# Summing kv over tokens in four column tiles, and moving query, keys and additions within a chunk: a tuned attention and GELU kernel on one core

## The chip, the cores and the metric

The kernel runs on one core of a Trainium2 chip. The metric is the device time of one execution in microseconds (us), the median of several. In what follows PE is TensorE (the matrix engine), DVE is VectorE, ACT is ScalarE, POOL is GpSimd and SP is SyncE, which here issues transfers. The time before is 283.5 us, the median of 3 runs (283.37 to 283.89). A run is called slow when it is over 1.5% above the fastest of its kernel.

## The reference, cut to what matters

Attention with sketched features, and behind it a two-layer network with exact GELU. All data is float32.

```python
# q, k, v: (4 batches, 4 heads, 1088 tokens, 32);  S1, S2: (8, 32)
def phi(x):                                   # 64 features of a token
    a = np.einsum('rd,bhsd->bhsr', S1, x)
    b = np.einsum('rd,bhsd->bhsr', S2, x)
    return np.einsum('bhsi,bhsj->bhsij', a, b).reshape(*x.shape[:-1], r * r)
q_p, k_p = (phi(q), phi(k))
kv = np.einsum('bhsf,bhsd->bhfd', k_p, v)
z = np.sum(k_p, axis=2)
num = np.einsum('bhsf,bhfd->bhsd', q_p, kv)
den = np.einsum('bhsf,bhf->bhs', q_p, z)[..., None] + 1e-06
x = (num / den)                               # rearranged to (4352 tokens, 128)
# then: h = x @ w_in (128 x 2048);  g = 0.5*h*(1+erf(h/sqrt(2)));  out = g @ w_out (2048 x 128)
```

## The kernel before

The kernel works through nine chunks of tokens: eight of 512 (two to a batch) and a half-wide one made of what is left over of the four batches. A chunk has 16 steps. A step is one *hidden* product (128 columns of `w_in`), its GELU on ACT, and *output* products with `w_out`. From chunk 2 on, the output products are of a cheaper form that adds up pieces in two accumulators (3.01 us of PE in the four steps from 128.86 to 135.31, against 0.86 us a step before chunk 2); POOL makes sums of GELU results for it (`token_sums`), and at the end of a chunk the accumulators are *drained* by DVE and ACT and put together by some additions on DVE (`combine`). Between these steps the attention of the chunks to come is worked in: a query is turned, expanded to features and multiplied with kv and z (`attend`), and the keys of a batch are turned, expanded and summed to kv and z.

kv and z before came from one product: `v_aug` holds v in 32 of 64 columns and ones in the others.

```python
def kv_sum(b, ps, r):
    for i in range(J):                                    # J = 8 groups of 128 tokens
        ch, t, one = (...)                                # cut: which slice of k_p
        for c in range(NP):                               # NP = 2
            pe.matmul(ps[c * 64:(c + 1) * 64, r * F:(r + 1) * F], lhsT=v_aug[:, 2 * c + r, i, :],
                      rhs=k_p[b, r][:, t, c * 4 + ch * 2 + one].rearrange("p i j -> p (i j)"),
                      start=(r == 0 and i == 0), stop=False, skip_group_check=True)

def combine(n):                                           # chunk n is complete
    dve.tensor_copy(out=N[:, 0], in_=acc[n][0])           # the drain ...
    act.copy(out=N[:, 1], in_=acc[n][1])
    act.copy(out=C[lo, 0], in_=flat[hi, HW:3 * HW])
    dve.tensor_add(...)                                   # ... and 7 additions, cut
```

The schedule names the step at which a part is issued. On each engine the instructions run in the order of this text.

```python
for b in range(1, B):
    t = NCH * b * NF - (0 if b == 1 else 1)               # NF = 16 steps, NCH = 2
    ...
    at(t - 18, key_turn_blocks, b, r)                     # for both r
    at(t - 17, features, b, r)
    t = NCH * b * NF - (0 if b == 1 else 2)
    at(t - 14, finish_keys, b)                            # kv_sum, and the copy to kv_T by DVE
    at(t - 13, lambda b=b: turn_kv(b, held["kv"], by_dve))   # the transpose of kv on PE
for n in range(2, NCHUNK):
    t = n * NF
    early = 0 if n == 2 else -1 if n == 3 else 2
    at(t - 13 - early, query_turn, n)
    at(t - 12 - early, query_expand, n)                   # half of the expansion ...
    at(t - 11 - early, expand_finish, n, 1)               # ... and the other half
    at(t - 8, attend, n)
# cut
    hidden(n, fi, ...)
    for n in done[t]:                                     # step 5 of the next chunk
        store(n)                                          # combine, transpose, stores
    token_sums(...)
    for f in slots[t]: f()
    for f, *a in products[t]: f(*a)
```

Of the kernel before, what the change touches and what calls it, by code (L numbers as in the profile page):

```python
# [16 lines left out]
def kernel(  # L17
# [21 lines left out]
    F = R * R  # L39
# [177 lines left out]
    kz = [big.tile([128, NP, 2 * D], FP, name=f"kz{b}") for b in range(B)]  # L217

    v_aug = big.tile([128, H, J, 2 * D], FP, name="v_aug")
# [9 lines left out]
    dve.memset(v_aug, 1.0)  # L229
# [81 lines left out]
    def widen_v(b, r):  # L311
        to = v_aug.rearrange("p (c r) j (s d) -> p c r j s d", r=2, s=2)[:, :, r, :, r, :]
        pool.tensor_copy(out=to, in_=main["v", b][:, r::2])

# [58 lines left out]
    def kv_sum(b, ps, r):  # L373

        for i in range(J):

            ch, t, one = (i % 2, i // 4, i // 2 % 2) if b else (i // 4, i // 2 % 2, i % 2)
            for c in range(NP):
                pe.matmul(ps[c * 64:(c + 1) * 64, r * F:(r + 1) * F], lhsT=v_aug[:, 2 * c + r, i, :],  # L379
                          rhs=k_p[b, r][:, t, c * 4 + ch * 2 + one].rearrange("p i j -> p (i j)"),  # L380
                          start=(r == 0 and i == 0), stop=False, skip_group_check=True)

    def kv_sum_rem(b, ps):
        for r in range(2):
            for c in range(NP):
                pe.matmul(ps[c * 64:(c + 1) * 64, r * F:(r + 1) * F], lhsT=v_rem_aug[b][:, 2 * c + r, :],
                          rhs=k_p_rem[b % 2][:, 2 * c + r].rearrange("p i j -> p (i j)"),
                          start=False, stop=True, skip_group_check=True)
# [56 lines left out]
    def expand_finish(n, i):  # L445
        for g in range(2):
            expand_copy(n, 2 * i + g)
        expand_multiply(n, i)

    def query_expand(n):  # L450
        expand_products(n)
        expand_finish(n, 0)

    def attend(n):

        W = width[n]
        owners = [(0, W, n // NCH)] if n < NMAIN else [(i * REM, (i + 1) * REM, i % 2 * 2 + i // 2) for i in range(B)]
        banks = halves(work_banks())
        for (c0, c1, b) in owners:
            for c in range(NP):  # L460
                for r in range(2):
                    pe.matmul(banks[r][c * F:(c + 1) * F, c0:c1], lhsT=kz[b][r * F:(r + 1) * F, c, :],  # L462
                              rhs=qp[n][r * F:(r + 1) * F, c, c0:c1], start=True, stop=True)
        den = att.tile([128, CW], FP, name="den")
        for h in range(H):
            c, r = h // 2, h % 2
            at = c * F + (1 - r) * D
            act.activation(out=den[h * D:(h + 1) * D, :W], in_=banks[r][at:at + D, :W], func=ACT.Copy, bias=1e-6)  # L468
        dve.reciprocal(out=den[:, :W], in_=den[:, :W])  # L469
        xT[n] = att.tile([128, CW], FP, name="xT", bufs=3)  # L470
        for h in range(H):
            rows = slice(h * D, (h + 1) * D)
            dve.tensor_mul(out=xT[n][rows, :W], in0=banks[h % 2][rows, :W], in1=den[rows, :W])  # L473
# [117 lines left out]

    def combine(n):

        N = att.tile([128, 2, CW], FP, name="A_sb", bufs=2)
        C = att.tile([128, 2, CW], FP, name="A_sb", bufs=2)
        dve.tensor_copy(out=N[:, 0], in_=acc[n][0])  # L596
        act.copy(out=N[:, 1], in_=acc[n][1])
# [69 lines left out]
    widen_v(0, 0)  # L667
# [3 lines left out]
    widen_v(0, 1)  # L671
# [9 lines left out]
    kv_sum(0, kv_bank, 0)  # L681
# [4 lines left out]
    kv_sum(0, kv_bank, 1)  # L686
# [59 lines left out]
    def finish_keys(b):  # L746
        held["kv"] = work_bank()
        for r in range(2):
            kv_sum(b, held["kv"], r)
# [16 lines left out]
    for b in range(1, B):  # L766

        t = NCH * b * NF - (0 if b == 1 else 1)
        for r in range(2):
            at(t - 20, widen_v, b, r)  # L770
        at(t - 20, widen_v_rem, b)
        for r in range(2):
            at(t - 18, key_turn_blocks, b, r)
        for r in range(2):
            at(t - 17, features, b, r)
        if b == 1:
            at(t - 16, turn_keys_rem, b)
            at(t - 15, features_rem, b)
        t = NCH * b * NF - (0 if b == 1 else 2)
        at(t - 14, finish_keys, b)  # L780
        at(t - 13, lambda b=b: turn_kv(b, held["kv"], by_dve))
    for n in range(2, NCHUNK):
        t = n * NF
        early = 0 if n == 2 else -1 if n == 3 else 2
        at(t - 13 - early, query_turn, n)
        at(t - 12 - early, query_expand, n)
        at(t - 11 - early, expand_finish, n, 1)
        at(t - 8, attend, n)
# [3 lines left out]
    done = {t: [] for t in range(len(steps) + LAG + 1)}  # L792
    for t, (n, fi) in enumerate(steps):
# [9 lines left out]
        elif fi % NB == NB - 1:  # L803
# [5 lines left out]
            if b == NF // NB - 1:  # L809
                done[t + 6].append(n)  # L810

    for t in range(len(steps) + LAG):
# [4 lines left out]
        if t == 4:  # L817
            turn_x(1, work_bank())
            for f, *a in products[t]:
                f(*a)  # L820
        if t < len(steps):
            n, fi = steps[t]
            hidden(n, fi, by_halves=n >= FAST and (n < NMAIN or fi < 5))
        for n in done[t]:
            store(n)
        if t < len(steps) and FAST <= steps[t][0] < NMAIN and steps[t][1] % NB == NB - 1:
            token_sums(steps[t][0], steps[t][1] // NB)
        for f in slots[t]:
            f()
        if t != 4:  # L830
# [43 lines left out]
```

## Time and profile before

The prediction below shows the main lines of this profile. This table cuts the span at starts of hidden products on PE.

| stretch | us |
|---|---|
| start, to the first hidden product | 18.57 |
| the next 24 steps (chunks 0 and 1 in turn), with kv of batch 1 | 47.36 |
| the last 8 steps of chunks 0 and 1, and chunks 2 and 3 | 74.12 |
| chunks 4 and 5 | 62.54 |
| chunks 6 and 7 | 55.88 |
| the last, narrow chunk and the tail | 22.93 |

How to read the lines: in a view in order of time, the columns are the start and the length in us, the engine, the line of the kernel, the operation, output and inputs, the tile or shape, and how many instructions were put together; a bracket at the end tells how long the engine had stood idle and what released it. SPq is SP's queue of transfers that it issues. Lengths of products overlap: the hidden product at 128.86 before is 1.03 us long, and the next group starts 0.86 us after it. Start-to-start distances are what PE pays.

In order of time on PE before, kv of batch 1, and the one large product that keeps PE busy in the start:

```profile
52.76 2.08 PE L379 MATMUL w_ps<-k_p,v_aug 128*64 128x64 f32 x64
54.67 0.40 PE L386 MATMUL w_ps<-k_p_rem,v_rem_aug 128*64 128x64 f32 x8
55.01 1.12 PE L624 MATMUL o_ps<-g,w_out 128*128 128x512 f32 x2
...
11.67 0.70 PE L653 MATMUL h_ps<-idle 128*128 128x256 f32 x2
```

kv of batch 1 takes 2.25 us from its first product to the next group (52.76 to 55.01).

### The profile page before, as it was taken

Reading aid. Unit: us, or ns where it says so; the run is one execution under the profiler, and the core shown is the slowest. Engines: PE = TensorE matmul, PEld = TensorE weight load, DVE = VectorE, ACT = ScalarE, POOL = GpSimd, SP = SyncE. Lnnn points to the kernel's source line nnn. Section 1 sums busy time; section 2 is a strip of 40 time slices with the busy share of each in tenths; the row PEclk is TensorE's granted clock in tenths of the full one; section 3 lists DMA queues with packets and bytes.
Section 4 is the critical chain, followed back from the end, with each engine's and each line's share of the span. In section 5 each row is a group of like instructions: output and inputs, shape, how many; then the busy total and the mean of one; then the engine's idle time right before and its main releaser. Section 6 shows DMA issues by size and latency. Waiting matters only on the chain.

```text
span 281.4 us, 5436 instructions
## 1 busy us (share of the span) xinstructions
PE 273.1 (97%) x2161; PEld 138.4 (49%) x2161; DVE 169.9 (60%) x244; ACT 141.1 (50%) x270; POOL 146.5 (52%) x160
## 2 busy tenths in 40 slices
PE   8989999999999999999999979999999999999994
PEld 6744444533432447444444446444544444455893
DVE  5987788253812394369816994379717971793050
ACT  4683864266426733466346532556355634553441
POOL 3331039002005858386767786286768676867500
PEclk9999999999999999999999999999999999999998
DMA  6559343626012100000200020000100020002011
GB/s 208 183 172 309 99 116 71 171 65 160 8 25 34 19 2 2 0 2 0 41 0 0 3 37 2 0 2 7 33 0 0 2 37 3 0 0 40 1 22 37
DMA packets 37914, 13.49 MB, mean 48 GB/s; under 512 B 28288, under 2 KB 37248, under 8 KB 37888
## 3 DMA queue, kind: packets, MB, share of 16 engines
q1 hardware_dynamic: 37648, 13.05, 18.2%
q8 instruction: 17, 0.28, 0.4%
q10 hardware_dynamic: 240, 0.08, 0.1%
q14 instruction: 9, 0.07, 0.1%
HBM read 10.90 MB, written 2.23 MB: 47 GB/s over the span
## 4 chain that ended last, share of the span: by engine, by line
PE 85%; DVE 9%; ACT 3%; issue 2%; DVEq 0%
PE h_ps L518 36%; PE o_ps L589 23%; PE o_ps L624 10%; PE w_ps L419 3%; PE w_ps L621 3%; PE w_ps L379 2%; PE w_ps L462 2%; ACT A_sb L426 2%; PE w_ps L653 1%; PE w_ps L345 1%; DVE den L469 1%; DVE q_pT L440 1%; DVE xT L473 1%; PE o_ps L379 1%; DVE A_sb L596 1%
## 5 line engine op out<-in xcount | busy, mean ns | idle before, releaser
L518 PE MATMUL h_ps<-xT,w_in 128*64 128x512 f32 (+3 forms) x490 | 140.2, 576 | 1.1 <-DVE xT L501 1.0
L525 ACT ACTIVATE block<-h_ps 128x512 f32<-128x512 f32 (+1 forms) x112 | 63.4, 566 | 89.3 <-PE h_ps L518 86.9
L560 POOL TENSOR_TENSOR bits_a<-block 128x512 f32<-128x512 f32 x24 | 30.9, 1287 | 68.6 <-ACT block L525 68.6
L518 PEld LDWEIGHTS h_ps<-xT,w_in 128*64 128x64 f32 (+1 forms) x490 | 44.1, 146 | 37.1 <-issue 16.8
L589 PE MATMUL o_ps<-block,w_out 128*64 128x256 f32 x192 | 50.9, 383 | 0.0
L440 DVE TENSOR_TENSOR q_pT<-A_sb,w_ps 64x512 f32<-64x512 f32 x32 | 22.1, 691 | 32.1 <-ACT A_sb L426 31.7
L589 PEld LDWEIGHTS o_ps<-block,w_out 128*64 128x64 f32 x192 | 25.0, 137 | 31.6 <-issue 24.6
L624 PE MATMUL o_ps<-g,w_out 128*128 128x512 f32 x64 | 33.4, 603 | 0.0
L563 POOL TENSOR_TENSOR bits_m<-block,bits_e 128x512 f32<-128x512 f32 x24 | 30.9, 1286 | 1.9
L562 POOL TENSOR_TENSOR bits_e<-bits_a,block 128x512 f32<-128x512 f32 x24 | 31.5, 1314 | 0.0
L561 POOL TENSOR_TENSOR bits_low<-block 128x512 f32<-128x512 f32 x24 | 31.5, 1312 | 0.0
L525 ACT ACTIVATE g<-h_ps 128x512 f32<-128x512 f32 x32 | 19.1, 596 | 24.2 <-PE h_ps L518 24.2
L469 DVE RECIPROCAL den<-den 128x512 f32<-128x512 f32 (+1 forms) x7 | 21.7, 3094 | 8.6 <-ACT den L468 8.6
L589 PE MATMUL o_ps<-bits_low,small 128*64 128x256 f32 x96 | 26.0, 383 | 0.0
L589 PE MATMUL o_ps<-block,small 128*64 128x256 f32 x96 | 24.9, 382 | 0.3
L589 PE MATMUL o_ps<-bits_a,small 128*64 128x256 f32 x96 | 25.0, 383 | 0.0
L589 PE MATMUL o_ps<-bits_m,w_out 128*64 128x256 f32 x96 | 25.0, 383 | 0.0
L589 PEld LDWEIGHTS o_ps<-block,small 128*64 128x64 f32 x96 | 12.7, 137 | 17.2 <-issue 9.1
L426 ACT COPY A_sb<-w_ps 64x512 f32<-64x512 f32 (+1 forms) x36 | 18.3, 554 | 3.2 <-PE w_ps L419 2.9
L473 DVE TENSOR_TENSOR xT<-w_ps,den 32x512 f32<-32x512 f32 (+1 forms) x28 | 18.2, 648 | 1.0
L624 PEld LDWEIGHTS o_ps<-g,w_out 128*128 128x128 f32 x64 | 11.3, 190 | 14.2 <-issue 13.3
L468 ACT ACTIVATE den<-w_ps 32x512 f32<-32x512 f32 (+1 forms) x28 | 15.6, 558 | 2.4 <-PE w_ps L462 2.0
(151 smaller groups left out, 317.4 us busy)
## 6 DMA issues: line engine op xcount, KB each, us to landing
block<-in_moe_w_in_dram SPq DMA_DIRECT2D x3, 512.0 KB, 6.6
block<-in_moe_w_out_dram SPq DMA_DIRECT2D x3, 512.0 KB, 9.6
k<-in_k_dram SPq DMA_DIRECT2D x48, 32.0 KB, 1.8
v<-in_v_dram SPq DMA_DIRECT2D x3, 512.0 KB, 4.5
q<-in_q_dram SPq DMA_DIRECT2D x24, 64.0 KB, 3.6
out_dram<-oT SPq DMA_DIRECT2D x24, 64.0 KB, 2.2
k<-in_k_dram SPq DMA_DIRECT2D x2, 256.0 KB, 3.1
q<-in_q_dram SPq DMA_DIRECT2D x2, 256.0 KB, 4.5
```

The lines of the kernel that those rows point to most:

```text
L426: act.copy(out=A[g // 2][F:, g % 2, :width[n]], in_=B_of[n][g // 2][:F, g % 2, :width[n]])
L440: dve.tensor_mul(out=cols[r * F:(r + 1) * F], in0=a[:, :, r::2], in1=b[:, :, r::2])
L469: dve.reciprocal(out=den[:, :W], in_=den[:, :W])
L473: dve.tensor_mul(out=xT[n][rows, :W], in0=banks[h % 2][rows, :W], in1=den[rows, :W])
L518: pe.matmul(ps[rows, :W], lhsT=w[:, rows], rhs=xT[n][:, :W], start=True, stop=True)
L525: act.activation(out=g_of[n, fi][:, :W], in_=ps[:, :W], func=ACT.Gelu)
L560: pool.tensor_add(out=s[1], in0=a21, in1=a22)
L561: pool.tensor_sub(out=s[3], in0=a11, in1=a21)
L562: pool.tensor_sub(out=s[2], in0=s[1], in1=a11)
L563: pool.tensor_sub(out=s[4], in0=a12, in1=s[2])
L589: pe.matmul(acc[n][bank][half * 64:(half + 1) * 64, col:col + HW], lhsT=fixed, rhs=moving, start=b == 0 and i in (0, 2), stop=b == NF // N ...
L624: pe.matmul(o_of[n], lhsT=w_tile(w_out_sb, fi), rhs=g, start=first, stop=final)
```

## The change

The intent has four parts. (1) kv is taken from v alone, in tiles of 32 columns, four beside each other on PE. z comes from ones times the features, and for batches 1 to 3 the features are first summed over groups of tokens (`add_tokens`, on POOL for batch 1 and on DVE for batches 2 and 3), so that fewer products of ones are needed. (2) The accumulators are drained ahead of the hidden product's GELU at step 5, and the additions come at step 11, last in it. (3) The numerators (`attend`) are at step 5 of every chunk, with the keys turned between them and the reciprocal. (4) The query is turned at step 1 and expanded wholly in step 2.

```diff
-    v_aug = big.tile([128, H, J, 2 * D], FP, name="v_aug")
+    ones = big.tile([128, D], FP, name="ones")
@@
+    def add_tokens(b, r, eng):
+        ... # cut: k_s[r] is k_p summed over its halves: 128x512, then 128x256
+        eng.tensor_add(out=..., in0=kp[:, 0]..., in1=kp[:, 1]...)
+        eng.tensor_add(out=k_s[r][:, :, 0], in0=k_s[r][:, :, 0], in1=k_s[r][:, :, 1])
+
+    def kv_sum(b, ps, heads, summed=False):
+        for i in range(J):
+            for add_ones in (False,) if summed else (False, True):
+                for h in heads:
+                    kv_product(ps, ones if add_ones else main["v", b][:, h, i, :], ...)   # 32 columns
+        if summed:
+            for m in range(2):
+                for h in heads:
+                    kv_product(ps, ones, k_s[r][:, c, 0, m], h, 2 * c + 1 - r)
@@ attend
+        meanwhile()                       # the keys are turned here
         dve.reciprocal(out=den[:, :W], in_=den[:, :W])
@@ the start, batch 0
-    kv_sum(0, kv_bank, 0)
+    kv_sum(0, kv_bank, range(0, H, 2))   # not summed: 64 products where there were 32 (both halves)
@@ the schedule
+    for n in range(3, NCHUNK):
+        t = (n - 1) * NF
+        keys = n % 2 and b < B
+        at(t + 1 if n > 3 else t - 3, query_turn, n)
+        at(t + 2 if n > 3 else t - 2, query_expand, n)
+        at(t + 5, attend, n, lambda b=b, keys=keys: [key_turn_blocks(b, r) for r in range(2) if keys])
+        if keys:
+            at(t + 10, features, b, r)
+            at(t + 10, add_tokens, b, r, dve)
+            at(t + 14, finish_keys, b)
+            at(t + 15, lambda b=b: turn_kv(b, held["kv"], by_dve))
@@
-                done[t + 6].append(n)
+                drains[t + 6].append(n)
+                done[t + 12].append(n)
@@ a step
+        for n in drains[t]:
+            drain(n)
         hidden(...)
-        for n in done[t]:
-            store(n)
         token_sums(...)
         for f in slots[t]:
             f()
+        for n in done[t]:
+            store(n)
```

More of the change, by code (lines that the diff above doesn't have):

```diff
@@ L228 @@
     dve.memset(idle, 0.0)
-    dve.memset(v_aug, 1.0)
+    dve.memset(ones, 1.0)
     class Rounding:
@@ L309 @@
     kT, k_p, k_p_rem, kv_T = {}, {}, {}, {}
-    def widen_v(b, r):
-        to = v_aug.rearrange("p (c r) j (s d) -> p c r j s d", r=2, s=2)[:, :, r, :, r, :]
-        pool.tensor_copy(out=to, in_=main["v", b][:, r::2])
     def widen_v_rem(b):
@@ L371, in key_features_rem @@
         dve.tensor_mul(**spread(k_p_rem[pair], a, ab[:, :, R:2 * R]))
-    def kv_sum(b, ps, r):
+    k_s = {}
+    def add_tokens(b, r, eng):
+        words = mlp.tile([128, LC], U32, name="bits_r")
+        k_s[r] = words.bitcast(FP).rearrange("p (c two one f) -> p c two one f", c=NP, two=2, one=2)
+        kp = k_p[b, r].rearrange("p t (c two one) i j -> p t c two one (i j)", c=NP, two=2)
+        eng.tensor_add(out=k_s[r].rearrange("p c two one f -> p (c two one f)"),
+                       in0=kp[:, 0].rearrange("p c two one f -> p (c two one f)"),
+                       in1=kp[:, 1].rearrange("p c two one f -> p (c two one f)"))
+        eng.tensor_add(out=k_s[r][:, :, 0], in0=k_s[r][:, :, 0], in1=k_s[r][:, :, 1])
@@ L375, in kv_sum, with kv_product @@
+    def kv_product(ps, lhsT, rhs, h, at, start=False, stop=False):
+        r = h % 2
+        pe.matmul(ps[at * D:(at + 1) * D, r * F:(r + 1) * F], lhsT=lhsT, rhs=rhs, start=start, stop=stop,
+                  skip_group_check=True)
+    def kv_sum(b, ps, heads, summed=False):
         for i in range(J):
             ch, t, one = (i % 2, i // 4, i // 2 % 2) if b else (i // 4, i // 2 % 2, i % 2)
-            for c in range(NP):
-                pe.matmul(ps[c * 64:(c + 1) * 64, r * F:(r + 1) * F], lhsT=v_aug[:, 2 * c + r, i, :],
-                          rhs=k_p[b, r][:, t, c * 4 + ch * 2 + one].rearrange("p i j -> p (i j)"),
-                          start=(r == 0 and i == 0), stop=False, skip_group_check=True)
@@ L383, in kv_sum_rem @@
-    def kv_sum_rem(b, ps):
-        for r in range(2):
-            for c in range(NP):
-                pe.matmul(ps[c * 64:(c + 1) * 64, r * F:(r + 1) * F], lhsT=v_rem_aug[b][:, 2 * c + r, :],
-                          rhs=k_p_rem[b % 2][:, 2 * c + r].rearrange("p i j -> p (i j)"),
-                          start=False, stop=True, skip_group_check=True)
+            for add_ones in (False,) if summed else (False, True):
+                for h in heads:
+                    c, r = h // 2, h % 2
+                    kv_product(ps, ones if add_ones else main["v", b][:, h, i, :],
+                               k_p[b, r][:, t, c * 4 + ch * 2 + one].rearrange("p i j -> p (i j)"),
+                               h, 2 * c + 1 - r if add_ones else h, start=i == 0 and (summed or r == 0))
@@ new lines, in kv_sum @@
+        if summed:
+            for m in range(2):
+                for h in heads:
+                    c, r = h // 2, h % 2
+                    kv_product(ps, ones, k_s[r][:, c, 0, m], h, 2 * c + 1 - r)
+    def kv_sum_rem(b, ps):
+        for s in range(2):
+            for h in range(H):
+                c, r = h // 2, h % 2
+                side = (r + s) % 2
+                kv_product(ps, v_rem_aug[b][:, h, side * D:(side + 1) * D],
+                           k_p_rem[b % 2][:, h].rearrange("p i j -> p (i j)"), h, 2 * c + side, stop=True)
@@ L443, in expand_multiply, with attend @@
                     dve.tensor_mul(out=cols[r * F:(r + 1) * F, g], in0=a[:, g, r::2], in1=b[:, g, r::2])
-    def expand_finish(n, i):
-        for g in range(2):
-            expand_copy(n, 2 * i + g)
-        expand_multiply(n, i)
     def query_expand(n):
         expand_products(n)
-        expand_finish(n, 0)
-    def attend(n):
+        for g in range(4):
+            expand_copy(n, g)
+            if g % 2:
+                expand_multiply(n, g // 2)
+    def attend(n, meanwhile=lambda: None):
         W = width[n]
@@ L590, in two_products, with drain, combine @@
                       start=b == 0 and i in (0, 2), stop=b == NF // NB - 1, skip_group_check=True)
-    def combine(n):
-        N = att.tile([128, 2, CW], FP, name="A_sb", bufs=2)
-        C = att.tile([128, 2, CW], FP, name="A_sb", bufs=2)
+    drained = {}
+    def drain(n):
+        N, C = (att.tile([128, 2, CW], FP, name="sums") for i in range(2))
         dve.tensor_copy(out=N[:, 0], in_=acc[n][0])
         act.copy(out=N[:, 1], in_=acc[n][1])
+        drained[n] = N, C
+    def combine(n):
+        N, C = drained[n]
         flat = N.rearrange("p a b -> p (a b)")
@@ L666 @@
     query_turn(0)
-    widen_v(0, 0)
     banks = [out_bank(), out_bank()]
@@ L670 @@
     key_features(0, 1, [hidden_bank(), hidden_bank()], by_pool=(1,))
-    widen_v(0, 1)
     widen_v_rem(0)
@@ L685 @@
     expand_multiply(0, 1)
-    kv_sum(0, kv_bank, 1)
+    kv_sum(0, kv_bank, range(1, H, 2))
     keep_busy(1, hidden_bank())
@@ L747, in finish_keys @@
         held["kv"] = work_bank()
-        for r in range(2):
-            kv_sum(b, held["kv"], r)
+        kv_sum(b, held["kv"], range(H), summed=True)
         kv_sum_rem(b, held["kv"])
@@ L765 @@
         at(22 + i, channel_sums, i)
-    for b in range(1, B):
-        t = NCH * b * NF - (0 if b == 1 else 1)
-        for r in range(2):
-            at(t - 20, widen_v, b, r)
-        at(t - 20, widen_v_rem, b)
-        for r in range(2):
-            at(t - 18, key_turn_blocks, b, r)
-        for r in range(2):
-            at(t - 17, features, b, r)
-        if b == 1:
-            at(t - 16, turn_keys_rem, b)
-            at(t - 15, features_rem, b)
-        t = NCH * b * NF - (0 if b == 1 else 2)
-        at(t - 14, finish_keys, b)
-        at(t - 13, lambda b=b: turn_kv(b, held["kv"], by_dve))
-    for n in range(2, NCHUNK):
-        t = n * NF
-        early = 0 if n == 2 else -1 if n == 3 else 2
-        at(t - 13 - early, query_turn, n)
-        at(t - 12 - early, query_expand, n)
-        at(t - 11 - early, expand_finish, n, 1)
-        at(t - 8, attend, n)
+    b, t = 1, NCH * NF
+    at(t - 20, widen_v_rem, b)
+    for r in range(2):
+        at(t - 18, key_turn_blocks, b, r)
+    for r in range(2):
+        at(t - 17, features, b, r)
+        at(t - 17, add_tokens, b, r, pool)
+    at(t - 16, turn_keys_rem, b)
+    at(t - 15, features_rem, b)
+    at(t - 13, finish_keys, b)
+    at(t - 12, lambda: turn_kv(1, held["kv"], by_dve))
+    at(t - 13, query_turn, 2)
+    at(t - 11, query_expand, 2)
+    at(t - 8, attend, 2)
+    for n in range(3, NCHUNK):
+        t = (n - 1) * NF
+        b = (n + 1) // 2
+        keys = n % 2 and b < B
[3 more added lines that the diff above has]
+        if keys:
+            at(t + 8, widen_v_rem, b)
+            for r in range(2):
+                at(t + 10, features, b, r)
+            for r in range(2):
+                at(t + 10, add_tokens, b, r, dve)
+            at(t + 14, finish_keys, b)
+            at(t + 15, lambda b=b: turn_kv(b, held["kv"], by_dve))
     products = {t: [] for t in range(len(steps) + LAG)}
     done = {t: [] for t in range(len(steps) + LAG + 1)}
+    drains = {t: [] for t in range(len(steps) + LAG + 1)}
     for t, (n, fi) in enumerate(steps):
```

## The prediction

> **What bounds the kernel now.** I read first the busy shares and slices, then the groups by form, then the order in time of each engine around every irregular stretch. The page of the kernel before:
>
> ```profile
> PE 273.1 (97%) x2161; PEld 138.4 (49%) x2161; DVE 169.9 (60%) x244; ACT 141.1 (50%) x270; POOL 146.5 (52%) x160
> ...
> PE   8989999999999999999999979999999999999994
> ...
> PEclk9999999999999999999999999999999999999998
> ```
>
> PE has work in every slice at full clock; the only dents are the ends and slice 24 (162 to 169 us). So only two kinds of change count: fewer PE cycles, or fewer waits of PE; plus the tail after its last matmul. DVE's 60% is an average: its deadlines inside a chunk of 512 tokens (about 29 to 32 us, 16 steps) decide. In order of time, PE shows what a step costs:
>
> ```profile
> 109.04 1.03 PE L518 MATMUL h_ps<-xT,w_in 128*64 128x512 f32 x4
> 109.90 2.04 PE L379 MATMUL w_ps<-k_p,v_aug 128*64 128x64 f32 x64
> 111.76 0.40 PE L386 MATMUL w_ps<-k_p_rem,v_rem_aug 128*64 128x64 f32 x8
> 112.00 0.38 PE L589 MATMUL o_ps<-block,w_out 128*64 128x256 f32 x1
> ```
>
> From start to start, a hidden product costs 0.86 us (109.04 to 109.90), kv of a batch 1.86 us and its remainder 0.24. That is 29 ns an instruction, in pairs of 64-column tiles. A pair of output products is 0.43. Elsewhere a hidden product ahead of another tile shape takes 0.96, and 0.05 is lost again on the way back.
>
> The stretch of slice 24, DVE and then PE:
>
> ```profile
> 161.32 3.31 DVE L469 RECIPROCAL den<-den 128x512 f32<-128x512 f32 x1
> 164.74 2.79 DVE L473 TENSOR_TENSOR xT<-w_ps,den 32x512 f32<-32x512 f32 x4
> 167.53 1.42 DVE L330 STREAM_TRANSPOSE kT<-k 128x256 f32<-128x256 f32 x4
> ...
> 165.53 1.03 PE L518 MATMUL h_ps<-xT,w_in 128*64 128x512 f32 x4
> 168.03 1.41 PE L345 MATMUL w_ps<-S,kT 64*64 64x32 f32 x64 [1.47 <-DVE kT L330]
> ```
>
> The keys of the last batch are turned behind the additions, reciprocal and xT. PE stands 1.47 us and does L345 in 1.34 in place of 1.06: 1.8 us lost with the switch. The other regular loss is the drain of the two accumulators between chunks:
>
> ```profile
> 149.45 1.89 PE L518 MATMUL h_ps<-xT,w_in 128*64 128x512 f32 x8
> ...
> 150.65 0.69 DVE L596 COPY A_sb<-o_ps 128x512 f32<-128x512 f32 x1
> ...
> 150.52 0.60 ACT L525 ACTIVATE block<-h_ps 128x512 f32<-128x512 f32 x1 [0.71 <-PE h_ps L518]
> 151.01 0.58 ACT L597 COPY A_sb<-o_ps 128x512 f32<-128x512 f32 x1
> ```
>
> ACT's drain stands behind a gelu and DVE's behind L440, so the next products start at 151.40, 1.95 after 149.45, where two hidden products need 1.72.
>
> [...]The trace agrees: 0.96 against 0.86 at a switch, and the four row tiles of L419 start 7 ns apart. Four column tiles appear nowhere in it. [...]The trace agrees strongly: the same addition L605 takes 1.38 us beside POOL and 0.42 at 268.94 when POOL is idle. [...]
>
> **The change part by part.**
>
> 1. kv. For batches 1 to 3, 32 products of v (64 instructions), 8 of ones on the token sums (16) and 8 of the remainder (16) make 96, where there were 72. A 64-column moving operand holds its tile for 58 ns (two tiles gave 29 ns an instruction). With four tiles: 96/4 x 58 ns = 1.40 us. Before it was 2.10 (2.25 for batch 1, which already had switches). Batches 2 and 3 now leave the 128x64 mode, +0.15 to 0.2 each. Gain 0.75 + 0.5 + 0.5 = **1.75 us**. Batch 0: 144 instructions at 14.6 ns, 2.1 us, as before: nothing. The POOL copies of v (0.61 to 0.67 each) and the 1.77 us memset go, but lie off the path.
>
> 2. Drains ahead of the hidden product's gelu, and all four multiplications of the query in step 2, so DVE is free too. Four boundaries (120.95, 149.45, 183.49, 211.99) lost 0.23, and 0.06 in the products behind. **Gain 1.15.** The fifth lost nothing.
>
> 3. Keys turned at step 5, ahead of the reciprocal: **gain 1.8.**
>
> 4. The sums of tokens are new DVE work for batches 2 and 3: per batch two additions 128x512 and two 128x256[...]. Clock from the end of hidden product 10 of that chunk. Features start at 0.1, and k_p ends 4.3 later (168.03 to 172.32 before), at 4.4. Gelu 11 stands behind the a_t copies, as it did at 171.50, so POOL starts its four sums at about 4.2[...]. Each addition then ends 0.3 (256 wide) or 0.55 (512) after the POOL one it waits behind, as L605 and L602 did: four take some 5.5 us, to about 10. PE gets there at: features 1.2, then products and hidden products of steps 10 to 14 (0.86 + 0.86 + 0.43 + 0.86 + 0.86 + 0.86 + 0.86 + 0.86), 7.7, and v's part 0.1 + 0.93, 8.75. A wait of about 1.2 us, twice: **loss 2.4.** Batch 1 has its sums on POOL and four steps of room: nothing.
>
> 5. The additions (combine) come at step 11, behind all this in DVE's order, and the kv copy for the transpose at step 15 comes behind them. There is no combine in batch 2's chunk; in batch 3's there is. DVE begins at 10, POOL being nearly idle until the last gelu: 3.6 us at the quiet durations, oT 0.71, kv copy 0.29, so 14.6. PE, through with kv at 10.5, needs 0.86 + 0.86 + 0.1 and stands there from 12.3. **Loss 2.2.** kz itself is not needed for another six steps; only the transpose's place in PE's order makes it a wait.
>
> 6. The tail. The last chunk is half as wide and its steps are only 0.87 us. Before:
>
> ```profile
> 267.34 0.68 DVE L602 TENSOR_TENSOR A_sb<-A_sb 64x512 f32<-64x512 f32 x1 [1.48 <-ACT A_sb L601]
> ...
> 271.00 0.71 DVE L635 STREAM_TRANSPOSE oT<-A_sb 128x512 f32<-128x512 f32 x1
> 277.26 0.29 DVE L630 COPY oT<-w_ps 128x128 f32<-128x128 f32 x1 [5.54 <-PE w_ps L621]
> ...
> 277.58 1.17 SPq L632 DMA_DIRECT2D out_dram<-oT  x2
> ```
>
> There were 5.5 us of room. Now the additions belong to step 11: gelu 11 ends at 272.8 on the old clock, ACT's copy (0.62) at 273.5, then DVE 4.4 us (267.34 to 271.71) to 277.9. The four stores of that chunk issue on SP at some 0.65 each (271.75, 272.36, 273.06, 273.74 before), to 280.5, and the last two outputs queue behind them: started at 277.58 and 278.15 before, now at 280.5 and 281.15. **Loss 2.7.**
>
> Sum: 283.5 - 1.75 - 1.15 - 1.8 + 2.4 + 2.2 + 2.7 = 286.1. The three losses rest on orders I traced by hand, each with a deadline that a little slack would soften, while the gains of 2 and 3 are nearly certain. I choose 285.3.
>
> **Rivals.** (a) The gains stand and the waits don't come: if POOL is late, DVE's sums take 2.2 us and end at 6.6, ahead of PE at 8.75, and items 4 and 5 nearly vanish: about 281.5 with the tail, 278.8 without it. For it: slice 24 shows exactly the DVE congestion that the change was made to remove. Against it: the additions beside POOL took 8.4 us in that very chunk (152.28 to 160.65). (b) Four column tiles don't run together, and an instruction stays at 29 ns: kv then costs 2.8 us for batches 1 to 3 and batch 0 twice what it did, some 4.5 us above item 1: about 290. For it: no four column tiles in the trace. Against: two column tiles and four row tiles overlap fully. (c) DVE is the bound of the whole chunk with keys: then the wait at the transpose grows to 4 us and the features' second bank, freed by xT at about the moment they start, costs PE some tenths: 288.
>
> **Range and chances.** The gains may miss by 1 us, items 4 and 5 by 2, the tail by 1; adding such independent misses gives about 2.5 either way: 282.5 to 288.0. Two per cent are 5.7 us: faster would need every loss to vanish and more, 0.02; slower would need rival (b) or (c) on top, 0.07; within, 0.91.
>
> **What would show it.** Item 1: kv's 96 instructions from first to last in about 1.4 us, without the wait. Item 2: 1.72 from the first of two hidden products to the next chunk's first products. Item 3: no idle before the features. Item 4: PE idle of about 1.2 before the products of ones, released by DVE, with POOL busy beside it. Item 5: PE idle of about 2.2 before one kv transpose, released by the DVE copy. Item 6: SP issues of the last full chunk running into the last two stores, and the end more than 6 us after the last matmul starts. I am wrong if DVE's additions fall into POOL's gaps, if tiles of 32 columns cost more than 15 ns, or if the last additions finish well ahead of the last matmul.

## More of the kernel before

The products of the start run without a gap.

## The result, and the profile after

The changed kernel takes 295.07 us, the median of 4 runs (293.17 to 295.88), beside 283.5 us for the kernel before in the same rounds. The ratio is 1.0396, 95% interval 1.0345 to 1.0448: slower by 4%. A ratio here is always the mean time of one kernel's fast runs over the mean of the other's fast runs of the same rounds, so it is not quite the ratio of the medians. The profiled executions lasted 281.4 us before and 294.1 us after. The prediction was 285.3, with a range that ended at 288.0.

The stretches of the table again, and a repaired version (experiment 9) to compare with later:

| stretch | before | after | after, repaired (e9) |
|---|---|---|---|
| start | 18.57 | 21.66 | 18.38 |
| next 24 steps | 47.36 | 46.59 | 46.60 |
| 8 steps, chunks 2 and 3 | 74.12 | 74.29 | 73.65 |
| chunks 4 and 5 | 62.54 | 68.59 | 60.46 |
| chunks 6 and 7 | 55.88 | 56.72 | 55.60 |
| last chunk and tail | 22.93 | 26.25 | 22.96 |

The whole loss of 12.7 us lies in the start (3.1), chunks 4 and 5 (6.1), chunks 6 and 7 (0.8) and the tail (3.3), with 0.2 more in the third row; 0.8 us was won in the second.

The busy shares and slices of the page after:

```profile
PE 277.5 (94%) x2305; PEld 139.6 (47%) x2305; DVE 179.3 (61%) x252; ACT 140.4 (48%) x270; POOL 150.4 (51%) x156
...
PE   8989999999999999999999975999999999999990
...
PEclk9999999999999999999999996999999999999997
```

PE's share fell from 97% to 94%. Slice 24 keeps its 7, and slice 25 is now a 5 with the granted clock down to 6 tenths. So PE stood there, and ran slowly. The list of waits of PE, in us in total, how often, and the longest, says for what:

```profile
PE w_ps L417 <- DVE kv_T L414: 4.9, 1, 4.9
PE w_ps L441 <- DVE qT L432: 1.2, 2, 0.6
...
PE w_ps L384 <- DVE bits_r L379: 0.7, 2, 0.3
PE w_ps L441 <- DVE qT_rem L432: 0.4, 1, 0.4
```

The transpose of kv of batch 3 waits 4.9 us, the query's products 1.2 + 0.4, and the products of ones on the sums of tokens 0.7. The old wait for turned keys (1.5 us) is gone. In order of time on PE, around that place:

```profile
162.93 1.20 PE L341 MATMUL w_ps<-S,kT 64*64 64x32 f32 x64
...
172.31 0.37 PE L384 MATMUL w_ps<-bits_r,ones 128*32 128x64 f32 x11 [0.33 <-DVE bits_r L379]
...
179.77 0.47 PE L417 MATMUL w_ps<-ident,kv_T 128*128 128x128 f32 x1 [4.94 <-DVE kv_T L414]
...
181.08 1.92 PE L539 MATMUL h_ps<-xT,w_in 128*64 128x512 f32 x4
```

The features (L341) now start without idle time. The hidden product at 181.08 takes 1.92 us where 1.03 is usual, because the clock was granted at half rate from 177.97 to 184.79. What DVE does in the meantime:

```profile
172.17 1.75 DVE L628 TENSOR_TENSOR sums<-sums 64x512 f32<-64x512 f32 x1
173.96 0.42 DVE L629 TENSOR_TENSOR sums<-sums 64x256 f32<-64x256 f32 x1
...
175.73 1.39 DVE L633 TENSOR_TENSOR sums<-sums 64x256 f32<-64x256 f32 x1
177.15 1.64 DVE L634 TENSOR_TENSOR sums<-sums 64x512 f32<-64x512 f32 x1
...
179.46 0.25 DVE L414 COPY kv_T<-w_ps 128x128 f32<-128x128 f32 x1
```

The copy of kv that PE waits for takes 0.25 us, but it stands behind the additions, which run from 172.17 to 178.8. On POOL at that time:

```profile
175.55 1.29 POOL L581 TENSOR_TENSOR bits_a<-block 128x512 f32<-128x512 f32 x1 [2.16 <-ACT block L546]
```

While POOL is idle (173.4 to 175.5) an addition of 64x256 takes 0.42 us. When POOL is back, the same shape takes 1.39. The first addition, of 64x512, ran beside the end of POOL's sums before (until 173.4) and took 1.75; one of that shape takes 0.69 when POOL is idle (experiment 9).

The drain after, at the beginning of chunk 4, again on PE. The numerators (L482) now lie between the two hidden products, and the next output products start 0.91 us after the second of them:

```profile
154.61 1.08 PE L539 MATMUL h_ps<-xT,w_in 128*64 128x512 f32 x4
...
155.52 0.38 PE L610 MATMUL o_ps<-block,small 128*64 128x256 f32 x1
```

The tail after, the issues of stores on SP (DVE has its last transpose for them from 287.02 on):

```profile
287.76 2.68 SPq L673 DMA_DIRECT2D out_dram<-oT  x4
290.53 1.21 SPq L658 DMA_DIRECT2D out_dram<-oT  x2
```

The four stores of the last full chunk are issued from 287.76 on and hold back the last two, which start at 290.53, 4.8 us after the last products' start at 285.75. kv of batch 1 after, with the group that follows:

```profile
57.57 1.10 PE L384 MATMUL w_ps<-k_p,v 128*32 128x64 f32 x64
58.48 0.41 PE L384 MATMUL w_ps<-bits_r,ones 128*32 128x64 f32 x16
58.71 0.41 PE L384 MATMUL w_ps<-k_p_rem,v_rem_aug 128*32 128x64 f32 x16
59.04 1.13 PE L650 MATMUL o_ps<-g,w_out 128*128 128x512 f32 x2
```

From 57.57 to 59.04 are 1.48 us (to the rounding of the starts) for 96 instructions, 15.4 ns each.

### The profile page after: what moved, and what is told of

The parts are those of the page before. It is cut to its first block, busy times and chain, and to the rows that moved or that the text cites. A ratio compares the mean times of both kernels' runs of the same rounds, so it can differ in the third digit from the quotient of the medians.

```text
span 294.1 us, 5722 instructions
## 1 busy us (share of the span) xinstructions
PE 277.5 (94%) x2305; PEld 139.6 (47%) x2305; DVE 179.3 (61%) x252; ACT 140.4 (48%) x270; POOL 150.4 (51%) x156
## 4 chain that ended last, share of the span: by engine, by line
PE 50%; POOL 19%; issue 18%; DVE 9%; ACT 2%; DVEq 0%; POOLq 0%
PE h_ps L539 21%; PE o_ps L650 10%; PE o_ps L610 8%; POOL bits_e L583 7%; POOL bits_m L584 6%; POOL bits_a L581 6%; PE w_ps L441 2%; PE w_ps L482 1%; PE w_ps L647 1%; PE w_ps L679 1%; DVE k_p L355 1%; PE o_ps L384 1%; DVE bits_r L379 1%; DVE bits_r L376 1%; DVE sums L634 1%
## 5 line engine op out<-in xcount | busy, mean ns | idle before, releaser
L539 PE MATMUL h_ps<-xT,w_in 128*64 128x512 f32 (+3 forms) x490 | 142.7, 581 | 1.1 <-DVE xT L522 1.0
L581 POOL TENSOR_TENSOR bits_a<-block 128x512 f32<-128x512 f32 x24 | 31.6, 1316 | 73.8 <-ACT block L546 73.8
L610 PE MATMUL o_ps<-block,w_out 128*64 128x256 f32 x192 | 51.7, 387 | 0.0
L610 PEld LDWEIGHTS o_ps<-block,w_out 128*64 128x64 f32 x192 | 25.9, 139 | 32.2 <-issue 25.0
L583 POOL TENSOR_TENSOR bits_e<-bits_a,block 128x512 f32<-128x512 f32 x24 | 34.5, 1436 | 0.0
L582 POOL TENSOR_TENSOR bits_low<-block 128x512 f32<-128x512 f32 x24 | 33.6, 1401 | 0.0
L610 PE MATMUL o_ps<-bits_m,w_out 128*64 128x256 f32 x96 | 25.6, 390 | 0.0
L628 DVE TENSOR_TENSOR sums<-sums 64x512 f32<-64x512 f32 x6 | 7.8, 1292 | 21.1 <-ACT sums L627 21.1
L448 ACT COPY A_sb<-w_ps 64x512 f32<-64x512 f32 (+1 forms) x36 | 17.7, 557 | 5.8 <-PE w_ps L441 5.7
## 6 DMA issues: line engine op xcount, KB each, us to landing
block<-in_moe_w_out_dram SPq DMA_DIRECT2D x3, 512.0 KB, 10.3
```

The costliest lines, as they stand in the source:

```text
L448: act.copy(out=A[g // 2][F:, g % 2, :width[n]], in_=B_of[n][g // 2][:F, g % 2, :width[n]])
L539: pe.matmul(ps[rows, :W], lhsT=w[:, rows], rhs=xT[n][:, :W], start=True, stop=True)
L581: pool.tensor_add(out=s[1], in0=a21, in1=a22)
L582: pool.tensor_sub(out=s[3], in0=a11, in1=a21)
L583: pool.tensor_sub(out=s[2], in0=s[1], in1=a11)
L610: pe.matmul(acc[n][bank][half * 64:(half + 1) * 64, col:col + HW], lhsT=fixed, rhs=moving, start=b == 0 and i in (0, 2), stop=b == NF // N ...
```

## The experiments

Eleven kernels ran, in three groups, each beside the kernel before on the same chip (its medians there: 283.57, 283.65 and 284.11 us). All gave correct results. After the theory of the first reading, PE's 4.9 us wait and the tail explain most of the loss. The rival is that they only stand in front of another limit.

**1. The transpose of kv two steps later.** Edit to the changed kernel:

```diff
-            at(t + 15, lambda b=b: turn_kv(b, held["kv"], by_dve))
+            at(t + 17, lambda b=b: turn_kv(b, held["kv"], by_dve))
```

> The changed kernel with one edit: the transpose of kv of batches 2 and 3 stands two steps later in PE's order (step 1 of the next chunk in place of step 15). Theory: the 4.9 us in which PE stood at this transpose, and the 6.8 us of half clock that followed (some 2.4 us lost), are both consequences of where the transpose stands; PE idle there falls under 0.5 us, the clock is not cut in the middle, and the time falls by 6.5 to 7.5 us against the changed kernel's 295 (to about 288). Rival: DVE is the bound of that chunk, and the wait turns up at the next DVE product (queries, keys): less than 3 us gained.

Measured: 291.12 us over all 6 runs (288.59 to 293.35), two of them slow; the four fast ones, the profiled one among them, took 288.59 to 291.58, ratio 1.0216 [1.0168, 1.0265]. Chunk 4 fell from 38.54 to 32.55 us, but chunk 5 rose from 30.05 to 32.28. The first line below is of this kernel's list of waits, the second of its PE in order of time:

```profile
PE w_ps L417 <- DVE kv_T L414: 1.9, 1, 1.9
```

```profile
14.48 0.48 PE L679 MATMUL h_ps<-idle 128*128 128x256 f32 x1 [2.56 <-issue]
```

Two steps were not enough: 1.9 us of the wait remained, and the clock was cut for 3.41 us once more (the hidden product at 180.44 takes 1.82 us where 1.03 is usual). So the place of the transpose sets the wait, but less was taken away than expected: 3.8 us over chunks 4 and 5, where 6.5 or more of time was expected. And this profile showed something new: in the start PE stands 2.56 us between two identical products, with no semaphore waited for ("issue").

**2. The last full chunk's additions and stores at once**, at the drain.

```diff
-                done[t + 12].append(n)
+                done[t + 6 if n == NMAIN - 1 else t + 12].append(n)
```

> The changed kernel with one edit: only the last full chunk's additions and store follow its drain at once (step 5 of the short chunk), as in the kernel before. Theory: the stores of that chunk hold up the last two in SP's order; the stretch from the last matmuls' group to the end falls back by 2.7 us (8.35 to about 5.7) and the time with it. Rival: the tail is longer for another reason (the last matmuls, the final copy): less than 1 us.

Measured: 294.42 us (293.15 to 295.66), ratio 1.0374 [1.0334, 1.0414]. In the profile the last stretch went from 26.25 to 23.60 us, 2.65 less, as expected. The spans of the two profiles differ by as much (294.1 and 291.4), but the medians (295.07 and 294.42, of different rounds) by less. Both kernels scatter by over 2 us from run to run, and which part of the runs takes up the rest was not traced.

**3. The additions of chunks 2, 4, 5 and 6 at step 8.**

```diff
-                done[t + 12].append(n)
+                done[t + 12 if n in (3, NMAIN - 1) else t + 9].append(n)
```

> The changed kernel with one edit: the additions of chunks 2, 4, 5 and 6 come at step 8 in place of 11 (that of chunk 3, beside the keys, and of the last stay). Theory: the additions end too late in DVE's order, and the next chunk's turned queries behind them; the three waits of PE ahead of the query products (0.69, 0.68 and 0.43 us) go, 1.8 us. Rival: the additions then collide more with GpSimd, slow its sums and make the output products wait: nothing gained.

Measured: 293.14 us over all 8 runs (290.84 to 297.33), ratio of the fast runs 1.0253 [1.0211, 1.0295]. Three of its runs were slow ones, the profiled one among them, so its trace is not used to explain a difference. What the expected 1.8 us rests on is shown by the next kernel, where the waits for qT are gone in a fast run. The ratio moved by more than those waits, 1.4%, and what the rest is stays open.

**4. All three together.**

> All three edits together. If the three losses are separate, the gains add up: 11 to 12 us, so about 283.5 with the late clock grant at the start, and some 3 us less in executions in which the clock is granted as early as in the kernel before. If the start's loss is made by the change it shows in every execution of all four kernels[...].

Measured: 285.45 us (284.04 to 287.01), ratio 1.0058 [1.0019, 1.0097]; span 284.5. The three edits give back 9 to 10 us of the loss of 11.6. No wait for qT or qT_rem is left in its list of waits. It still has 2.0 us at the transpose of kv, 0.7 for the sums of tokens, and 2.1 of "issue" in the start. Its six runs give neither one value nor two groups: 284.0 and 284.3 us at a mean granted clock of 1.000, 285.4 and 285.5 at 0.994, 286.2 and 287.0 at 0.987 and 0.988.

**5. Batch 0 alone in the old form.** The start has no semaphore to blame. But kv of batch 0 has 144 product instructions there where it had 72, since z of batch 0 is not summed beforehand. This kernel is the changed one with `v_aug` and the 64-wide products back for batch 0 only.

```diff
-    kv_sum(0, kv_bank, range(0, H, 2))
+    kv_wide(0, kv_bank, 0)               # v beside ones, 64 columns, as before
@@
-    kv_sum(0, kv_bank, range(1, H, 2))
+    kv_wide(0, kv_bank, 1)
# cut: v_aug filled with ones by DVE, v copied into it by POOL, the remainder in the old form
```

> The changed kernel, but batch 0's kv in the old form (v widened by GpSimd, 64-column tiles: 72 product instructions in place of 144). Theory: the start loses[...]: with the new form it stands some 2.5 us with nothing to wait for. With the old form the first hidden product starts at about 18.6 us again (21.1 to 23.6 in the changed kernel's family), and the time falls by about 3 us from 295, to 292. Rival: [...]then the start stays late in some executions, and the median moves by less than 1 us.

Measured: 292.07 us (291.38 to 292.98), ratio 1.0288 [1.0256, 1.0319]: 3 us better than the changed kernel. The first hidden product starts at 18.22, and the runs lie closer together (1.6 us from lowest to highest, where the changed kernel has 2.7).

**6. More instructions in the kernel before.** To tell the number of instructions from the form of the products, the old kernel gets 36 tiny products (72 product instructions, and as many weight loads) at that place, which read only zeros.

```diff
-    keep_busy(1, hidden_bank())
+    spare = hidden_bank()
+    for i in range(36):
+        pe.matmul(spare[i % 4 * 32:(i % 4 + 1) * 32, CW - 16:], lhsT=idle[:, 0:32], rhs=idle[:, :16], ...)
+    keep_busy(1, spare)
```

> The kernel before with 36 tiny products (72 instructions, as many as the new kv of batch 0 adds, 16 columns wide, on zeros) put in front of batch 0's remainder, the result thrown away. Their own work is about 0.5 us. [...]PE stands 2 to 3 us more with no wait named, the first hidden product starts at 21 us or later, and the time rises by 2.5 to 4 us over 283.5. Rival: the number of instructions doesn't matter, and the start's loss comes from the 32-column tiles or from the clock: then at most 0.7 us.

Measured: 285.45 us (284.99 to 288.09), ratio 1.0078 [1.0034, 1.0123]; the first hidden product comes at 20.75, 2.18 us later. That is below the expected range and well above the rival's. On its PE, in order of time:

```profile
11.57 0.74 PE L689 MATMUL h_ps<-idle 128*32 128x16 f32 x65
13.69 0.25 PE L689 MATMUL h_ps<-idle 128*32 128x16 f32 x7 [1.38 <-issue]
```

The row of equal products breaks after the 65th. Counted from the beginning, the break lies behind the 221st product on PE. In kernels 1, 2 and 4, whose instructions there are different ones, it lies behind the 221st product too, and so it does in kernel 10. The kernels that come to the 222nd product only at 14.1 us or later (before, 5, 7, 8, 9, 11) show no gap. So at this place the number of instructions matters, whatever the form of the products: 72 tiny ones made a gap of 1.38 us, as the new kv of batch 0 made gaps of 2.56, 1.69, 2.08 and 1.82 us (kernels 1, 2, 4 and 10). What PE stands for in the gap was not shown: the trace names no semaphore.

**7. A first repair**: kernel 4, batch 0 in the old form, kv at step 15, and its copies by ACT instead of DVE.

```diff
-        take_kv(b, held["kv"], by_dve)
+        take_kv(b, held["kv"], by_dve if b == 1 else by_act)
@@
-            at(t + 14, finish_keys, b)
-            at(t + 17, lambda b=b: turn_kv(b, held["kv"], by_dve))
+            at(t + 15, finish_keys, b)
+            at(t + 17, lambda b=b: turn_kv(b, held["kv"], by_act))
```

> The three edits of the last batch with batch 0's kv in the old form, kv of batches 2 and 3 finished one step later (15), and its two copies on ScalarE in place of VectorE. If the causes found so far are all there is: start at 18.6 (3.9 us better than the kernel with three edits in its profile), the remaining wait at the transpose of 2.0 us and the two waits for the token sums of 0.65 us each gone: 284.5 - 3.9 - 2.0 - 1.3 = 277.3 us of span, about 279 us of time, faster than before's 283.5 by 1.5 per cent. Rival: DVE is simply full in the last batch's chunk, and the wait comes up elsewhere: about 281.5.

Measured: 283.75 us (281.62 to 284.70), ratio 0.9977 [0.9937, 1.0017], span 281.9. My theory missed the span by 4.6 us, and the rival's 281.5 was near it. The wait had moved, as this line of PE in order of time shows:

```profile
177.95 2.09 PE L465 MATMUL w_ps<-qT,Srep 32*128 32x512 f32 x8 [2.79 <-DVE qT L456]
```

With the copy of kv off DVE, the next thing behind the additions in DVE's order is the turn of the next query. PE waits 2.79 us for it, and the clock is at half rate from 177.91 to 181.32 (the output products there take 0.63 us each, from 181.31 on 0.39).

**8. The new schedule with the old kv for every batch**: no sums over tokens, no tiles of 32 columns.

```diff
-        kv_sum(b, held["kv"], range(H), summed=True)
+        for r in range(2):
+            kv_wide(b, held["kv"], r)
@@
-                at(t + 10, add_tokens, b, r, dve)
# cut: v copied between ones by POOL (batches 2 and 3 at step 8), batch 0 as in kernel 5, no add_tokens for batch 1
```

> The changed kernel with the whole kv of before (v widened, 64-column tiles, no sums of tokens), so that only the new schedule is left. Theory: the start is that of before (-3.1 us), no waits for sums (-1.3), DVE is 5 us earlier in the last keys' chunk, so that the wait at the transpose (4.9) and the clock cut behind it (2.4) go or nearly go; kv itself costs 1.5 us more. The waits ahead of the queries (1.8) and the tail (2.7) stay. About 285. Rival: the schedule alone, not the sums, makes the wait at the transpose: then it stays above 3 us, the clock is still cut, and the time is 290 or more.

Measured: 286.60 us (286.33 to 286.86), ratio 1.0093 [1.0066, 1.0121]; span 284.9. That is 1.6 us above the expectation and clear of the rival's 290. So the new kv with its sums, in this schedule, costs 8.5 us, of which 3 are the start's (kernel 5). Its wait at the transpose of kv, from the list of waits:

```profile
PE w_ps L441 <- DVE kv_T L438: 1.2, 1, 1.2
```

Without the sums over tokens ahead of them on DVE, the same additions let the copy through 3.7 us earlier as PE sees it, and the clock is not cut in the middle. They are no faster there (7.3 us, 164.69 to 172.0, four of them slow beside POOL); they begin 4.7 us earlier in the chunk. In return the waits for qT and the tail (26.24 us) are as in the changed kernel, so those belong to the schedule.

**9. The additions of chunk 3 behind the turn of the next query**, to take out what was left in kernel 7.

```diff
-  done[t + 6 if n == NMAIN - 1 else t + 12 if n == 3 else t + 9].append(n)
+  done[t + 6 if n == NMAIN - 1 else t + 18 if n == 3 else t + 9].append(n)
```

> e7_repaired with one number changed: the additions of chunk 3 (the accumulators that are drained within the chunk that turns batch 3's keys) come after the turn of the next query, in the chunk behind, instead of at step 11. Theory: what was left in e7_repaired is the same work on DVE in a third place: the additions at the slow rate end at 176.6, the query turn behind them at 177.9, and PE stands 2.8 us ahead of the query's products and then runs 3.4 us at half clock (about 1.6 us lost). With the additions behind the query turn both go: chunk 5 falls from 33.1 to 28.3-28.7 us, span 277.2-277.8, median 279-279.8 us, ratio about 0.985. Rival: DVE is short of time in that stretch wherever the additions stand; the wait then comes back at the product q_pT or at the next drain, and the span stays at 280 or above.

Measured: 279.57 us (279.26 to 279.87), ratio 0.9841 [0.9815, 0.9867], span 277.7: 1.6% faster than the kernel before, under 2% but with an interval clear of 1. The first line is of its page, the other two are its whole list of waits of PE:

```profile
PE 271.0 (98%) x2233; PEld 137.9 (50%) x2233; DVE 167.2 (60%) x250; ACT 141.4 (51%) x274; POOL 148.8 (54%) x158
```

```profile
PE w_ps L703 <- DVE idle L228: 1.2, 1, 1.2
PE h_ps L563 <- DVE xT L546: 1.0, 1, 1.0
```

Both are in the start and were there before. The additions now run from 173.95 to 177.6, where POOL is idle: 3.7 us in place of 6.65. DVE's busy time fell from 179.3 to 167.2 us for nearly the same instructions.

**10. The changed kernel once more**, to see what of the loss is in every execution.

> The changed kernel once more, unaltered, to see which parts of its loss are in every execution. Theory: the wait of PE at the kv transpose of batch 3 (4.9 us) and a cut of the clock after it, the waits ahead of the query's products (1.3 to 1.8 us in all) and the tail (2.7) come again to 0.2 us; the start differs: the first hidden product comes 2.0-5.0 us after the old 18.57, either through a gap of PE of 1.4-2.9 us with no semaphore waited for, or through a clock granted late. Median 293-296. Rival: if the late clock of the first profile is a thing of this kernel and not of chance, the clock is again granted only at 13-15 us and there is no gap.

Measured: 295.61 us (294.37 to 297.05), ratio 1.0407 [1.0362, 1.0453]. The wait of 4.9 us, the waits for qT and qT_rem (1.2 and 0.4) and the last stretch (26.25) came again. The start differed from that of the first profile. On PE in order of time:

```profile
13.34 0.48 PE L679 MATMUL h_ps<-idle 128*128 128x256 f32 x1 [1.82 <-issue]
```

Here the gap is there, as in kernel 1, and the first hidden product comes at 21.14. In the first profile of the changed kernel it came at 21.66 without a gap, because the full clock was granted only at 14.13 us (at 5.17 here, at 6.75 before): a product of kv takes 0.32 us until 14.0 there, and 0.23 at 10.3 here. PE reached its 222nd product only at 15.11. The four other fast profiles with the same instructions in the start (1, 2, 4 and 10) have the full clock at 4.10 to 7.14 us and all have the gap. So the late clock of that one profile did not come again in these four, and it hid the gap.

**11. Kernel 9 with the old kv for every batch**, to see what the new kv is worth where nothing waits for it.

> e9_sums_after_query with kv in the old 64-wide form for every batch (v beside ones, no sums over tokens), all else the same: the difference of the two is what the new kv is worth by itself where nothing waits for it. Theory (item 1 of the prediction, as measured at batch 1): 96 instructions in 1.48 us against 72 in 2.10 to 2.25, with a switch of 0.1 to 0.2 more for the new form: 0.75 us for batch 1 and 0.4 to 0.5 for batches 2 and 3, so this kernel's span is 1.4-1.8 us above e9's. Rival: the sums over tokens still cost DVE time that shows elsewhere, and the two kernels are the same within 0.7 us or this one is the faster.

Measured: 281.86 us (281.59 to 282.12), ratio 0.9919 [0.9890, 0.9947], span 280.3. The medians differ by 2.3 us and the profiled spans by 2.7, more than the 1.4 to 1.8 expected. By stretches, 1.15 us lie in the 24 steps with batch 1 (0.77 of them in kv itself, 2.25 against 1.48), 0.3 and 0.36 in the chunks with batches 2 and 3: 1.8 us in the stretches where kv is taken. The rest, 0.4 in the start and 0.5 in the last chunk, has nothing to do with these products, and its cause was not sought.

## Why the prediction was wrong

**Item 1, kv: right for batches 1 to 3, wrong for batch 0.** The instruction took 15.4 ns against 14.6 foreseen (29 in two tiles before), and the gain where nothing waits is 0.77 + 0.30 + 0.36 = 1.4 us against 1.75. Rival (b) fell. The step that failed is "Batch 0: 144 instructions at 14.6 ns, 2.1 us, as before: nothing". I counted time and not instructions. With the doubled number PE stood 1.69 to 2.56 us, with no semaphore named, in the start of kernels 1, 2, 4 and 10, and in three of these four half rate followed for 3.41 or 6.83 us (in kernel 1 it did not). The start lost 3.1 us in the first profile, where a late clock hid the gap, and 2.6 in kernel 10. Kernels 5 and 6 show from both sides that the number matters (3 us won, 2.18 lost); why it does was not shown.

**Items 2 and 3, drains and keys: right.** The two hidden products at the drain take 0.96 and 0.91 us now (152.63 to 153.59, 154.61 to 155.52). These 1.87 us hold the 0.10 and 0.05 of a change of tile shape that was paid elsewhere before, so it is 1.72 without them. The 12 products behind take 1.29 in place of 1.35. The features start without idle time and take 1.13 us to the next group, with the switch. Both are read from the trace; no run undid one of them alone.

**Item 4, waits for the sums of tokens: right in kind, too large.** I had 1.2 us each; kv of batch 3 took 2.11 us from start to start against 1.48 without a wait, so about 0.65. The sums were done at 172.17, 9.3 us on the prediction's clock, where I had 10.

**Item 5, the kv transpose: the main miss.** The failed term is "3.6 us at the quiet durations, POOL being nearly idle until the last gelu". I took this although the same additions had taken 8.4 us beside POOL in that chunk before, a number that I gave against rival (a). They took 6.65 us: the first ran beside the end of POOL's sums before, and POOL took up its last four at 175.55, in the middle of them. With the start 0.7 earlier, the copy of kv ended at 179.7, 16.9 us on that clock instead of 14.6, and PE was there at 12.0: 4.94 us in place of 2.2. Rival (c) had named a wait of 4 us. That the sums over tokens are what pushed the additions there is shown by kernel 8 (wait 1.2 us, with additions as slow). That POOL causes the slow ones is read from which durations coincide; no run took POOL's work away.

The prediction had no term for what followed: the clock. In the trace, half rate was granted for 6.83 us, of which PE worked 5.0 (179.77 to 184.79), so an estimated 2.5 us were lost; in kernel 10 it was 3.41 us and so an estimated 1.7. Shorter waits were followed by half rate too: one of 2.79 us (kernel 7) and one of 1.95 (kernel 1) by 3.41 us of it, while one of 2.0 (kernel 4) was not. Rival (c) had a wait of 4 us, and I priced no slower clock there.

**A step that was missing: the query behind the additions.** I followed DVE's order only as far as the kv copy. In the chunks without keys the turn of the next query stands there. The additions of chunk 2 run beside POOL from 137.14 to 146.2, and the query's products wait for qT until 147.63, behind a hidden product that starts at 145.98: the hidden products ahead of the query's took 1.65, 1.64 and 1.39 us instead of 0.96 in three chunks, 1.8 us in all. These waits were gone with the additions at step 8 (kernel 4).

**Item 6, the tail: right.** The group from the last products to the end took 8.35 us against 5.68 before: 2.67, and kernel 2 gave 2.65 of it back. That the figure fits so well is in part luck: the prediction's own lines put the last stores at 280.5 where they had been at 277.58, which is 2.9 and not 2.7. In item 5, too, 14.6 less 12.3 is 2.3 and not 2.2.

The sum, redone for the profile with what was measured: 281.4 - 1.4 - 1.15 - 1.8 + 1.3 (item 4) + 4.9 + 2.5 (clock) + 1.8 (query) + 2.7 (tail) + 3.1 (start) = 293.4, against a span of 294.1. What is missing, 0.7 us, includes the narrow chunk's wait for its query (0.4). The direction of the choice was wrong as well: I took 0.8 us off my own sum, because slack would soften the losses.

## What to carry to other kernels

When work on a secondary engine is moved, follow that engine's order past the first consumer to everything behind it, and use the durations measured beside the busy neighbour: here the same seven additions took 3.7 us or 6.65 depending on where they stood, and their wait moved from kv to the query until they stood behind both. A wait of the matrix engine should be priced with the slower clock that may follow: here half rate for 3.41 to 6.83 us came behind waits of 1.95, 2.79 and 4.94 us, and none behind one of 2.0. And a form that needs more instructions for the same work can cost time in the first microseconds even where it keeps the engine no longer busy: 72 tiny products moved the first hidden product by 2.18 us here.
